# A residual stored to the output early, an MLP result added by accumulating DMA, left sums of the first token blocks made a stage earlier, and a fifth product of two levels

## The chip, the cores and the metric

The kernel runs on one core of one Trainium2 chip. A core has TensorE (matrix products into PSUM, in eight banks of 128 x 512 float32), VectorE, ScalarE, GpSimd (POOL in the profile), and SyncE (SP), whose instruction queue issues nearly all DMA transfers here. Each engine works through its own queue in order; semaphores tie the queues together. The metric is the time of one execution on the device in microseconds. Three runs of the kernel before took 742.08 to 745.21 us, with a median of 743.17.

## The reference

One transformer block over 2048 tokens of width 1024, all inputs bfloat16: layer norm, linear attention with 32 heads, a residual, layer norm, a gated MLP of width 3584, and a second residual.

```
h   = x + A(layernorm(x))                       # linear attention, output projection wo
n   = layernorm(h)
act = relu(n @ W_gate) * (n @ W_up)             # 2048 x 3584
out = h + act @ W_down                          # 2048 x 1024
```

`h` is needed twice: its normalised form feeds the MLP, and `h` itself is added to the MLP's result at the end.

## The kernel before

**Products of seven.** Every large product is cut into 2 x 2 blocks and done with seven block products in place of eight (Winograd's form of Strassen's scheme): sums and differences of left blocks, the same of right blocks, seven products, and sums of those give the four output blocks. A left operand with blocks a11, a12, a21, a22 (first index: half of the tokens, second index: half of the summed dimension) needs s1 = a21 + a22, s2 = s1 - a11, s3 = a11 - a21 and s4 = a12 - s2; products 1 to 7 have the left forms a11, a12, s4, a22, s1, s2, s3. The class `Quad` (L302) holds the steps of one such group of seven, p1 to p7, and `Quads` (L357) runs one group after the other, with products 4 and 3 of a group placed inside the next one. VectorE makes the sums and takes results out of PSUM, ScalarE copies between PSUM banks ("fork") and to SBUF ("snap").

**Tokens.** 2048 tokens are two halves of 1024, the row blocks of the scheme. Each half is again two blocks of 512 tokens, numbered `s` = 0 and 1. The MLP's width is two halves of 1792, each of `FH` = 14 chunks of 128; the output's width is two halves of 512.

**Stages.** (1) Attention, up to about 217 to 280 us, overlapping the next stage. It makes h tile by tile and stores each to a DRAM scratch tensor `h_dram` (`square`, L1009 to L1017). (2) The up stage: for each chunk `fc` and each `s`, one group of seven (`gu_quad`, L1085) gives four blocks of act, 128 x 512 each, for the two token halves and the two halves of the width. A group is 56 matmuls of 128 x 512. The blocks of s = 0 stay in SBUF (`hh0`, L1082). Those of s = 1 go, together with their sums s1 to s4, to DRAM (`spill`, L1097, into `l_dram`), since SBUF has no room for both. In the second half of this stage VectorE also makes the sums of W_down's blocks chunk by chunk (`wd_sums`, L1195), loads them and stores them to `r_dram` through two sets of buffers. (3) The down stage, from about 582 us: the seven products of act with W_down, in the order 1, 2, 6, 5, 7, 3, 4 (L1428 to L1440).

**The down stage.** Each of its seven products has 1024 tokens (both `s`), 1792 summed and 512 columns. A *shallow* one (`shallow`, L1311) does it plainly: 2 blocks `s`, 4 tiles of 128 tokens, 14 chunks, so 112 matmuls of 128 x 512. A *deep* one (`deep`, L1345) applies the seven-product scheme once more inside: the two `s` are its row halves, the tokens are taken in two groups `g`, and each group has seven products of 2 tiles x 7 chunks, 98 matmuls of 128 x 256. For it VectorE makes four right sums (`inner_rights`, L1324) and four left sums per group (`inner_lefts`, L1335), all 128 x 1792. `DEEP` (L1245) names products 2, 3, 5 and 6. Before a product, its right operand (`right`, 1792 KB, two buffers in turn) and the left operand of s = 1 (`left`, 1792 KB, two buffers in turn) are loaded by SP. The left operand of s = 0 comes from `hh0`; where a sum is wanted, `sums0` (L1305) makes it on VectorE in the down stage: eight instructions of 128 x 3584 in all, for s1, s3, s2 and s4, in place or into a free region.

Running sums are kept in SBUF as float32: `U` from products 1, 6 and 7, `Y` from product 5. Four products end an output quarter `q`: product 2 (q = 0), 7 (q = 3), 3 (q = 1) and 4 (q = 2). In each, `load_h` brings the matching 128 KB of h from `h_dram` (32 loads), h is added, and `store` writes 128 KB to the output through SP (32 stores). In products 2 and 3 VectorE adds h to the base (`keep` and `onto`), in product 7 inside `seven`, and in product 4 ScalarE copies h into the PSUM bank ahead of the matmuls (`seed`).

**What sets the order.** All instructions after the set-up are recorded by `Plan` (L33) and then put out in an order that a planner works out from costs and due times written in its code (`cost`, `take`, `schedule`). TensorE keeps near its program order; for SP and VectorE the planner takes what is ready and due first. So an edit in one place can move instructions of these two queues elsewhere. Each queue is fixed once built. Every instruction is issued through L117, which is why all groups of the profile bear that line; they are told apart by tile and shape.

```
            limit = nodes[pe[first]].nom + self.WINDOW
            i = min(now, key=lambda i: (nodes[i].nom if e == "tensor" else nodes[i].late, i))
```

Of the kernel before, what the change touches and what calls it, by code (L numbers as in the profile page):

```python
# [32 lines left out]
class Plan:  # L33
# [30 lines left out]
    def granules(self, ap):  # L64
        key = (ap.tensor.name, ap.offset, ap.ap, ap.dtype)
        if key not in self.cache:
            (row, _), *dims = ap.ap
            size = self.nbytes(ap)
            starts = [ap.offset % row]
            for step, n in dims[:-1]:  # L70
                starts = [s + step * i for s in starts for i in range(n if step else 1)]
            step, n = dims[-1]
            span = step * (n - 1) + 1
            g = 4 if ap.tensor.name.startswith("tiny") else self.G
            self.cache[key] = (ap.tensor.name, sorted({
                q for s in starts for q in range(s * size // g, ((s + span) * size - 1) // g + 1)}))
        return self.cache[key]
# [12 lines left out]
    def cost(self, eng, op, out, ins, k):  # L90

        n = self.free(out)
        if eng == "tensor":
            return max(n / 2.4, 98.0) if op == "matmul" else 80.0, 160 + self.SEM
        if eng == "sync":
            return (1250.0 if op == "dma_start_transpose" else 500.0), self.wire(out) + 2200.0
        acc = 85.0 if k.get("accum_out") is not None else 0.0
        psum = any(a.space == PSUM for a in ins)
        if eng == "vector":
            narrow = all(self.nbytes(a) == 2 and a.space != PSUM for a in (out, *ins) if self.free(a) > 1)  # L100
            mode = {"tensor_tensor": 2, "tensor_scalar": 4, "memset": 2}.get(op, 1) if narrow else 1
            if ins:
                n = max(n, self.free(ins[0]))
            return n / (0.96 * mode) + 69 + acc, 95 + self.SEM
        if eng == "scalar":
            return n / 1.2 + (51 if psum else 93) + 2 * acc, 105 + self.SEM
        return n * 1.15 + 100, 60 + self.SEM

    def take(self, eng, op, args, k):
# [5 lines left out]
        accumulates = op == "matmul" and not k.get("start", True)  # L115
# [3 lines left out]
        if nodes and nodes[-1].open and op == "matmul":  # L119
            v = nodes[-1]  # L120
            v.hold += hold
        else:
            v = Plan.Node()
            v.eng, v.calls, v.preds, v.hold, v.lat, v.dma = eng, [], set(), hold, lat, 0.0
            if eng == "sync":
                v.dma = self.wire(out)
            nodes.append(v)
# [327 lines left out]
def block_kernel(ctx: ExitStack, tc: tile.TileContext, x, wqkv, wo, wg, wu, wd, out, H: int):  # L455
    nc = tc.nc
# [29 lines left out]
    h_dram = dram.tile([P, ST, D], BF16, name="h_dram")  # L486

    LT = {m: BF16 if m in (1, 2, 4) else FP16 for m in range(1, 8)}
    l_dram = {m: dram.tile([P, FH, SW], LT[m], name=f"l_dram{m}") for m in range(1, 8)}
    r_dram = {m: dram.tile([P, FH, D // 2], FP16, name=f"r_dram{m}") for m in (4, 5, 6, 7)}  # L490
# [463 lines left out]
    class Tile_:  # L954
# [54 lines left out]
        def square(self):  # L1009
            h = self.h  # L1010
            nc.sync.dma_start(out=h_dram[:, self.t, :], in_=h)
# [72 lines left out]

    def gu_quad(s, fc, gw, banks):  # L1085
# [10 lines left out]

        def spill():  # L1097

            (a11, a12, a21, a22), (s1, s2, s4) = hh1, ss1
            s3 = a21.bitcast(FP16)  # L1100
            for o, x, y, op in ((s1, a21, a22, ALU.add), (s2, s1, a11, ALU.subtract),
                                (s3, a11, a21, ALU.subtract), (s4, a12, s2, ALU.subtract)):
                nc.vector.tensor_tensor(out=o, in0=x, in1=y, op=op)
            for m, f in ((2, a12), (6, s2), (5, s1), (7, s3), (3, s4), (4, a22)):
                nc.sync.dma_start(out=l_dram[m][:, fc, :], in_=f)
# [16 lines left out]
        def added(q):  # L1122
            def f(ps, u):
# [5 lines left out]
                if s == 1 and q == 1:  # L1129
                    spill()  # L1130
# [85 lines left out]
    for n, (s, fc) in enumerate(order):  # L1216
# [14 lines left out]
        if 8 <= n < 8 + FH:  # L1231
            wd_sums(n - 8)
        if n == 24:
# [11 lines left out]
    DEEP = (2, 3, 5, 6)  # L1245
# [6 lines left out]
    h_ring = ring_of([190.5 + i for i in range(3)])  # L1252
    o_ring = ring_of([193.5 + i for i in range(2)])
    m_ring = ring_of([195.5 + 2 * i for i in range(4)])
# [22 lines left out]
    def load_h(q, s, tt, n, lo, width):  # L1277
        y = at(h_ring(), [n, width])
        t = tile_no(q, s, tt)
        lo += q % 2 * DW  # L1280
        nc.sync.dma_start(out=y, in_=h_dram[:, t:t + n, lo:lo + width])
        return y

    def store(q, s, tt, lo, width, o):
        t = tile_no(q, s, tt)
        lo += q % 2 * DW
        nc.sync.dma_start(out=of_v[:, t:t + o.shape[1], lo:lo + width], in_=o)
# [17 lines left out]
    def sums0(o, x, y, op):  # L1305

        for g in range(2):
            c = slice(g * 2 * P, (g + 1) * 2 * P)
            nc.vector.tensor_tensor(out=o[:, :, c], in0=x[:, :, c], in1=y[:, :, c], op=op)

    def shallow(m, r, lefts, order, then, seed=None):  # L1311
        for s in order:
            for tt in range(4):
                b = shallow_bank()
                if seed is not None:
                    nc.scalar.copy(out=b, in_=load_h(seed, s, tt, 1, 0, DW)[:, 0, :])
                for f in range(FH):
                    if f == FH - 1:
                        nc.cut()
                    nc.tensor.matmul(b, lhsT=lefts[s][f][:, tt * P:(tt + 1) * P], rhs=r[:, f, :],  # L1320
                                     start=(seed is None and f == 0), stop=(f == FH - 1), skip_group_check=True)
# [23 lines left out]
    def deep(m, r, x1, src, dst=None, q=None, with_h=None):  # L1345
# [4 lines left out]
        def quad(g):  # L1350
            lefts = inner_lefts(L0[m], x1, g)

# [7 lines left out]
            def end(s, v, ps, x):  # L1360
                if q is None:
                    add(dst(s, v, g), pair(ps), x)
                else:
                    o = at(o_ring(), [2, DQ])
                    add(o, pair(ps), x)
                    store(q, s, 2 * g, v * DQ, DQ, o)

            def base(s, v):
                return src(s, v, g) if q is None else with_h(src(s, v, g), q, s, v, g)

            def usnap(A, which):
                b = base(which, 1)
                o = b if q is not None else dst(which, 1, g)
# [10 lines left out]
    def keep(src, q, s, v, g):  # L1384
        o = at(m_ring(), [2, DQ], FP32)
        add(o, src, load_h(q, s, 2 * g, 2, v * DQ, DQ))
        return o

    def onto(src, q, s, v, g):
        add(src, src, load_h(q, s, 2 * g, 2, v * DQ, DQ))  # L1390
        return src
# [5 lines left out]
    def seven(s, tt, b):  # L1397
        add(UM[:, s, tt, :], b, UM[:, s, tt, :])
        h = load_h(3, s, tt, 1, 0, DW)
        o = at(o_ring(), [1, DW])  # L1400
        for v in range(2):
            c = slice(v * DQ, (v + 1) * DQ)
            m = at(m_ring(), [2, DQ], FP32)[:, 0, :]
            add(m, Y(s, v, tt // 2)[:, tt % 2, :], h[:, 0, c])
            add(o[:, 0, c], b[:, c], m)
        store(3, s, tt, 0, DW, o)

    def step(m, src, dst=None, q=None, with_h=None):
        r, z = right(m), left(m)
        if m in DEEP:  # L1410
            deep(m, r, z, src, dst, q, with_h)
# [4 lines left out]
        def then(s, tt, b):  # L1416
# [5 lines left out]
            if q is not None:  # L1422
                store(q, s, tt, 0, DW, o.unsqueeze(1))

        shallow(m, r, [[a[:, f, :] for f in range(FH)] for a in (L0[m], z)], (0, 1),
                seven if m == 7 else then, q if m != 7 else None)

    sums0(L0[5], lq[2], lq[3], ALU.add)  # L1428
    sums0(L0[7], lq[0], lq[2], ALU.subtract)
    step(2, U, q=0, with_h=keep)  # L1430

    sums0(L0[6], L0[5], lq[0], ALU.subtract)
    step(6, U, U)
    sums0(L0[3], lq[1], L0[6], ALU.subtract)
# [4 lines left out]
    step(3, Y, q=1, with_h=onto)  # L1439
    step(4, U, q=2, with_h=onto)  # L1440
# [53 lines left out]
```

## Time and profile before

| | |
|---|---|
| median of three runs | 743.17 us (742.08 to 745.21) |
| the profiled execution's own time | 744.89 us |
| its span in the profile | 743.1 us |
| TensorE busy, matmuls | 722.2 us, 3858 |
| VectorE busy | 531.8 us |
| ScalarE busy | 278.6 us |
| POOL busy | 43.7 us, all before 300 us |
| bytes moved by DMA | 110.01 MB in 138707 packets |
| granted TensorE clock | 0.998 of full speed |
| small store to the output, from issue to landing | 1.8 us median, 32 of 128 KB |
| small load of h | 2.4 us median, 32 of 128 KB, 11.9 at most |
| left operand of 1792 KB from l_dram | 7.5 us median |
| right operand of 1792 KB from r_dram | 8.9 us median |

The span is what the profiler saw on the core; the execution's own time is a little longer than the span. A row of the timeline or of the groups gives the engine, the operation, the output and inputs with their shapes (partitions x elements), and in brackets how long the engine stood idle before it and what ended that idle time. A row of a stretch gives its length and each engine's busy time with the number of instructions in it. A few matmul records are missing from the trace, so counts of them are slightly low. Consecutive VectorE instructions of 16-bit operands overlap a little, so that a group's busy time is somewhat below count times mean.

### The profile page before, as it was taken

To read this page: it belongs to the slowest core of one execution; us is meant where nothing else is said; L and a number is where in the kernel's file an instruction comes from. 1 tells how busy PE (TensorE), PEld (TensorE's weight loads), DVE (VectorE), ACT (ScalarE), POOL (GpSimd) and SP (SyncE) were. 2 spreads that over 40 slices of the span, in tenths; PEclk is the share of its full clock that TensorE was granted. 3 is DMA by queue.
4 is the path that set the end of the run, shared out by engine and by line. 5 is a ranking of instruction groups with operands and counts; after the bars stand their busy time and mean duration, and the time that the engine had idled before them with its cause. 6 is when DMAs were issued, how large, how long until landed. Compare 5 with 4: busy or idle time off the path is not lost.

```text
span 743.1 us, 10494 instructions
## 1 busy us (share of the span) xinstructions
PE 722.2 (97%) x3858; PEld 371.7 (50%) x3911; DVE 531.8 (72%) x893; ACT 278.6 (37%) x542; POOL 43.7 (6%) x62
## 2 busy tenths in 40 slices
PE   8899999999999999999999999999998999999998
PEld 3344545444444444444444444444443468884763
DVE  6887755786987875676647546668755999997942
ACT  6677645656554443333323233332323110000010
POOL 2223000002201110000000000000000000000000
PEclk9999999999999999999999999999999999999999
DMA  9464503069856630436051141675876854446741
GB/s 302 105 132 86 170 1 127 3 144 266 189 131 152 140 71 8 140 118 203 21 146 53 43 135 37 183 244 172 258 255 224 270 199 135 174 191 244 266 131 52
DMA packets 138707, 110.01 MB, mean 148 GB/s; under 512 B 54176, under 2 KB 126368, under 8 KB 137248
## 3 DMA queue, kind: packets, MB, share of 16 engines
q1 hardware_dynamic: 138656, 109.34, 50.4%
q8 instruction: 30, 0.49, 0.3%
q14 instruction: 21, 0.17, 0.1%
HBM read 68.68 MB, written 28.57 MB: 131 GB/s over the span
## 4 chain that ended last, share of the span: by engine, by line
PE 64%; DMA 4%; DVE 2%; issue 1%; SPq 1%; ACT 0%; DVEq 0%; ACTq 0%
PE psum L117 64%; DMA mem<-in_B_W_down_dram 2%; DVE mem L117 2%; DMA r_dram<-mem 1%; DMA l_dram<-mem 1%; SPq L117 1%; ACT mem L117 0%; DVEq L1489 0%; DVEq L117 0%; ACTq L117 0%
## 5 line engine op out<-in xcount | busy, mean ns | idle before, releaser
L117 PE MATMUL psum<-mem 128*128 128x512 f16 (+4 forms) x3842 | 721.1, 348 | 16.0 <-DVE mem L117 5.9
L117 PEld LDWEIGHTS <-mem 128*128 128x128 f16 (+1 forms) x3911 | 371.7, 98 | 367.3 <-issue 15.5
L117 DVE TENSOR_TENSOR mem<-psum,mem 128x1024 bf16<-128x1024 f32 (+3 forms) x252 | 185.2, 753 | 143.3 <-ACT mem L117 81.5
L117 DVE TENSOR_TENSOR mem<-mem 128x512 f16<-128x512 bf16 (+8 forms) x332 | 207.4, 663 | 15.4 <-DMA mem<-in_B_W_down_dram 5.2
L117 ACT COPY mem<-psum 128x512 f32<-128x512 f32 (+2 forms) x120 | 90.4, 754 | 209.5 <-PE psum L117 199.7
L117 ACT COPY psum<-psum 128x512 f32<-128x512 f32 (+1 forms) x62 | 45.7, 736 | 154.6 <-PE psum L117 132.3
L117 ACT ACTIVATE mem<-psum 128x512 bf16<-128x512 f32 x90 | 53.6, 597 | 17.9 <-PE psum L117 17.0
L117 DVE SCALAR_TENSOR_TENSOR mem<-mem 128x512 bf16<-128x512 bf16 (+1 forms) x71 | 58.0, 817 | 1.4
L117 DVE SCALAR_TENSOR_TENSOR mem<-psum,mem 128x512 bf16<-128x512 f32 x66 | 45.4, 688 | 15.4 <-PE psum L117 10.3
L117 POOL TENSOR_SCALAR mem<-mem,tiny 128x1024 bf16<-128x1024 bf16 x30 | 38.0, 1266 | 191.9 <-ACT tiny L117 143.2
L117 DVE TENSOR_SCALAR mem<-mem 128x512 bf16<-128x512 bf16 (+1 forms) x49 | 19.3, 393 | 24.4 <-ACT mem L117 24.1
L117 ACT ACTIVATE mem<-mem,tiny 128x1024 bf16<-128x1024 bf16 x25 | 28.6, 1145 | 14.1 <-DVE tiny L117 8.2
L117 ACT ACTIVATE mem<-mem 128x1024 bf16<-128x1024 f32 (+1 forms) x24 | 25.3, 1055 | 4.9 <-DVE mem L117 3.8
L117 ACT ACTIVATE tiny<-tiny 128x1 f32<-128x1 f32 (+2 forms) x112 | 22.3, 206 | 7.8 <-DVE tiny L117 5.1
L117 DVE TENSOR_TENSOR mem<-psum,tiny 128x384 bf16<-128x384 f32 (+1 forms) x48 | 22.8, 507 | 2.6 <-ACT tiny L117 2.0
L117 ACT ACTIVATE tiny<-psum 128x12 f32<-128x12 f32 (+1 forms) x48 | 8.1, 171 | 16.2 <-PE psum L117 16.0
L117 ACT CAST psum<-mem 128x512 f32<-128x512 bf16 x8 | 4.7, 590 | 24.4 <-DMA mem<-h_dram 13.3
L117 ACT CAST mem<-psum 128x512 bf16<-128x512 f32 x18 | 10.5, 582 | 3.2 <-PE psum L117 2.5
L117 DVE BATCH_NORM_STATS2 tiny<-mem 128x6 f32<-128x512 bf16 x14 | 9.2, 678 | 2.2 <-DMA mem<-in_A_x_dram 2.2
L117 POOL TENSOR_SCALAR tiny<-tiny 128x1 f32<-128x1 f32 x14 | 4.2, 300 | 36.7 <-ACT mem L117 23.4
L117 ACT ACTIVATION_READ_ACCUMULATOR mem<-mem,tiny 128x1 f32 x25 | 4.7, 188 | 0.0
L117 DVE TENSOR_SCALAR tiny<-tiny 128x1 f32<-128x1 f32 x16 | 3.4, 211 | 0.4
(18 smaller groups left out, 13.5 us busy)
## 6 DMA issues: line engine op xcount, KB each, us to landing
l_dram<-mem SPq DMA_DIRECT2D x98, 128.0 KB, 2.2
mem<-l_dram SPq DMA_DIRECT2D x6, 1792.0 KB, 7.5
mem<-in_A_x_dram SPq DMA_DIRECT2D x32, 256.0 KB, 3.1
mem<-in_B_W_gate_dram SPq DMA_DIRECT2D x14, 512.0 KB, 4.1
mem<-in_B_W_up_dram SPq DMA_DIRECT2D x14, 512.0 KB, 5.2
mem<-in_B_W_down_dram SPq DMA_DIRECT2D x28, 256.0 KB, 3.5
r_dram<-mem SPq DMA_DIRECT2D x56, 128.0 KB, 2.6
mem<-r_dram SPq DMA_DIRECT2D x4, 1792.0 KB, 8.9
```

The lines of the kernel that those rows point to most:

```text
L117: call = lambda: getattr(getattr(self.nc, eng), op)(*args, **k)
```

## The change

1. **h goes to the output.** `square` stores each tile of h to the output tensor in place of `h_dram`, which is gone. `load_h`, where it is still used, reads it from there.
2. **Results are added by DMA.** `store` has a new argument. With it set, GpSimd issues a DMA that adds the bfloat16 result to what the output holds (`accum_op=ALU.add`); without it, SP stores as before. All results of products 2, 7 and 3 and those of group 0 of product 4 are added this way, 28 transfers of 128 KB. Group 1 of product 4 still loads h (4 loads), adds it on VectorE and stores plainly (4 stores). `keep`, `onto` and the seeding of PSUM are gone; in product 2 the snap writes to a scratch tile (`scratch_u`).
3. **Left sums of s = 0 are made in the up stage.** `spill` takes `s` and is called for both. For s = 0 it makes the four sums of each chunk (4 instructions of 128 x 512), leaves s3 in place of a21, and stores s1, s2 and s4 to the new DRAM tensors `s_dram` 5, 6 and 3 (3 x 14 stores of 128 KB). Chunks 0 to 3, which are made in another way early in the stage, get theirs at turns 9 to 12. In the down stage `left0` loads each of the three back (1792 KB), and `sums0` is gone.
4. **Product 4 becomes deep**, as the fifth.
5. Rings are resized: h buffers 3 to 2, result buffers 2 to 5, scratch 4 to 3. The planner learns the cost of a GpSimd DMA, that an accumulating one reads its target, and to tell rows of a DRAM tensor apart.

The diff, cut to its core:

```diff
@@ Plan
-            starts = [ap.offset % row]
+            starts = [ap.offset % row + ap.offset // (128 * row) * (128 * row)]
...
+        if op == "dma_start" and eng == "gpsimd":
+            return 1000.0, 2.0 * self.wire(out) + 4500.0
...
-        accumulates = op == "matmul" and not k.get("start", True)
+        accumulates = k.get("accum_op") is not None or op == "matmul" and not k.get("start", True)
@@ square
-            nc.sync.dma_start(out=h_dram[:, self.t, :], in_=h)
+            nc.sync.dma_start(out=of[self.t * P:(self.t + 1) * P, :], in_=h)
@@ up stage
+    s_dram = {m: dram.tile([P, FH, SW], FP16, name=f"s_dram{m}") for m in (3, 5, 6)}
...
+    def spill(s, fc):
+        a11, a12, a21, a22 = (hh0(q, fc) if s == 0 else hh1[q] for q in range(4))
+        s1, s2, s4 = ss1
+        s3 = a21.bitcast(FP16)
+        for o, x, y, op in ((s1, a21, a22, ALU.add), (s2, s1, a11, ALU.subtract),
+                            (s3, a11, a21, ALU.subtract), (s4, a12, s2, ALU.subtract)):
+            nc.vector.tensor_tensor(out=o, in0=x, in1=y, op=op)
+        if s == 0:
+            for m, f in ((5, s1), (6, s2), (3, s4)):
+                nc.sync.dma_start(out=s_dram[m][:, fc, :], in_=f)
+        else:
+            for m, f in ((2, a12), (6, s2), (5, s1), (7, s3), (3, s4), (4, a22)):
+                nc.sync.dma_start(out=l_dram[m][:, fc, :], in_=f)
...
-                if s == 1 and q == 1:
-                    spill()
+                if q == 1:
+                    spill(s, fc)
...
+        if 9 <= n < 13:
+            spill(0, n - 9)
@@ down stage
-    DEEP = (2, 3, 5, 6)
+    DEEP = (2, 3, 4, 5, 6)
...
-    h_ring = ring_of([190.5 + i for i in range(3)])
-    o_ring = ring_of([193.5 + i for i in range(2)])
-    m_ring = ring_of([195.5 + 2 * i for i in range(4)])
+    h_ring = ring_of([190.5 + i for i in range(2)])
+    o_ring = ring_of([192.5 + i for i in range(5)])
+    m_ring = ring_of([197.5 + 2 * i for i in range(3)])
...
-    def store(q, s, tt, lo, width, o):
+    def store(q, s, tt, lo, width, o, onto_h):
         t = tile_no(q, s, tt)
         lo += q % 2 * DW
-        nc.sync.dma_start(out=of_v[:, t:t + o.shape[1], lo:lo + width], in_=o)
+        dst = of_v[:, t:t + o.shape[1], lo:lo + width]
+        if onto_h:
+            nc.gpsimd.dma_start(out=dst, in_=o, accum_op=ALU.add)
+        else:
+            nc.sync.dma_start(out=dst, in_=o)
...
-    def sums0(o, x, y, op):
-        for g in range(2):
-            c = slice(g * 2 * P, (g + 1) * 2 * P)
-            nc.vector.tensor_tensor(out=o[:, :, c], in0=x[:, :, c], in1=y[:, :, c], op=op)
+    def left0(m):
+        nc.sync.dma_start(out=L0[m], in_=s_dram[m][:, :, :])
...
-                if seed is not None:
-                    nc.scalar.copy(out=b, in_=load_h(seed, s, tt, 1, 0, DW)[:, 0, :])
...
+            with_h = last and g == 1
...
-                    store(q, s, 2 * g, v * DQ, DQ, o)
+                    store(q, s, 2 * g, v * DQ, DQ, o, not with_h)
...
             def base(s, v):
-                return src(s, v, g) if q is None else with_h(src(s, v, g), q, s, v, g)
+                x = src(s, v, g)
+                if with_h:
+                    add(x, x, load_h(q, s, 2 * g, 2, v * DQ, DQ))
+                return x
...
-            m = at(m_ring(), [2, DQ], FP32)[:, 0, :]
-            add(m, Y(s, v, tt // 2)[:, tt % 2, :], h[:, 0, c])
-            add(o[:, 0, c], b[:, c], m)
-        store(3, s, tt, 0, DW, o)
+            add(o[:, 0, c], b[:, c], Y(s, v, tt // 2)[:, tt % 2, :])
+        store(3, s, tt, 0, DW, o, True)
...
-    sums0(L0[5], lq[2], lq[3], ALU.add)
-    sums0(L0[7], lq[0], lq[2], ALU.subtract)
-    step(2, U, q=0, with_h=keep)
-    sums0(L0[6], L0[5], lq[0], ALU.subtract)
+    left0(5)
+    step(2, U, scratch_u, q=0)
+    left0(6)
     step(6, U, U)
-    sums0(L0[3], lq[1], L0[6], ALU.subtract)
+    left0(3)
     step(5, U, Y)
     step(7, U)
-    step(3, Y, q=1, with_h=onto)
-    step(4, U, q=2, with_h=onto)
+    step(3, Y, Y, q=1)
+    step(4, U, U, q=2, last=True)
```

## The prediction

> **What bounds the kernel now.** I read the busy shares first, then the stretches of the down stage, then TensorE's own timeline, then what VectorE did ahead of the one gap.
>
> ```profile
> PE 722.2 (97%) x3858; PEld 371.7 (50%) x3911; DVE 531.8 (72%) x893; ACT 278.6 (37%) x542; POOL 43.7 (6%) x62
> ```
>
> TensorE is busy 97% of the span. An edit pays only if it takes TensorE work away or closes one of its gaps; VectorE, ScalarE and DMA count where TensorE waits for them. The stretches below are cut where a product of the down stage should begin, worked back from the last matmul at 739.5 (columns: stretch, length, busy PE, weight loads, DVE, ACT, POOL with counts, granted clock, DMA share, GB/s).
>
> ```profile
> 581.90:606.10 24.20, 24.10 (x120) 11.73 (x121) 24.01 (x23) 4.73 (x9) 0.00 (x0) 1.00 0.68 229
> 606.10:627.20 21.10, 21.10 (x195) 18.88 (x194) 18.85 (x23) 1.67 (x3) 0.00 (x0) 1.00 0.42 137
> 627.20:648.20 21.00, 21.00 (x195) 18.77 (x193) 19.59 (x23) 1.14 (x2) 0.00 (x0) 1.00 0.51 197
> 648.20:669.30 21.10, 21.08 (x191) 18.41 (x189) 18.91 (x27) 0.57 (x1) 0.00 (x0) 1.00 0.54 199
> 669.30:693.50 24.20, 24.20 (x117) 11.25 (x116) 20.78 (x42) 0.00 (x0) 0.00 (x0) 1.00 0.61 211
> 693.50:715.30 21.80, 21.02 (x186) 17.95 (x184) 17.89 (x26) 2.19 (x4) 0.00 (x0) 1.00 0.74 254
> 715.30:739.60 24.30, 24.20 (x120) 11.43 (x117) 6.54 (x17) 3.67 (x7) 0.00 (x0) 1.00 0.27 84
> ```
>
> These are products 1, 2, 6, 5, 7, 3, 4. A shallow one (1, 7, 4) takes 24.2 us, a deep one 21.0 to 21.1, and TensorE is full in all but the sixth, though VectorE is at 18 to 24 us in each but the last. POOL does nothing. The two gaps inside are these:
>
> ```profile
> 561.12 150.21 PE L117 MATMUL psum<-mem 128*128 128x512 f16 x1064 [2.70 <-ACT mem L117]
> 712.11 27.39 PE L117 MATMUL psum<-mem 128*128 128x256 f16 x140 [0.78 <-DVE mem L117]
> ```
>
> Ahead of the first, ScalarE's copy at 560.06 waited 6.01 us for VectorE, and VectorE's own queue shows why; ahead of the second it sat on a load of h:
>
> ```profile
> 555.25 0.76 DVE L117 TENSOR_TENSOR mem<-mem 128x512 f16<-128x512 bf16 x2 [2.21 <-DMA mem<-in_B_W_down_dram]
> 555.93 0.68 DVE L117 TENSOR_TENSOR mem<-psum,mem 128x512 bf16<-128x512 f32 x1
> 557.03 0.42 DVE L117 TENSOR_TENSOR mem<-mem 128x512 f16<-128x512 bf16 x1 [0.42 <-DMA mem<-in_B_W_down_dram]
> 558.07 0.76 DVE L117 TENSOR_TENSOR mem<-mem 128x512 f16<-128x512 bf16 x2 [0.61 <-DMA mem<-in_B_W_down_dram]
> ...
> 707.44 0.69 DVE L117 TENSOR_TENSOR mem<-mem 128x512 f32<-128x512 f32 x1 [1.56 <-DMA mem<-h_dram]
> ```
>
> In its fixed order VectorE stands before weight sums whose loads have not landed: 2.21 + 0.42 + 0.61 = 3.24 us late, of which TensorE feels 2.70.
>
> **Product 4 made deep.** It drops 8 x 14 = 112 matmuls of 128x512 and issues 2 groups x 7 products x 2 tiles x 7 chunks = 196 of 128x256. Wide: an up-stage quad is 56 matmuls in 12.09 us on the chain (one begins at 318.47, the next at 330.56), 215.9 ns each. Narrow: 21.0 us over the 195 recorded in the third stretch, 107.7 ns. So 24.18 becomes 21.11: **-3.1 us**. Two rules of one page bear on this. The Trainium skill's "TensorE: Matmul & The Clock Gate", section "Back-to-back issue gap", says that a stream of weight load and matmul runs at about 131 ns for 512 columns and 81 for 128; at those paces (an estimate) 112 wide ones would take 14.7 us and 196 narrow ones at least 15.9, and the edit would lose over 1 us. Its isolated gap, 518 cycles against 262 at 2.4 GHz, gives 24.2 against 21.4, -2.8. This trace contradicts the first pair and agrees with the second; I take the trace's own rows. The 84 extra weight loads stay under the matmuls: deep stretches hold 18.4 to 18.9 us of them in 21.
>
> VectorE's share of product 4 grows: 12 sums of 128x1792 at 1.083 us (4 right, 8 left) = 13.0, 12 evacuations of 128x512 at 0.685 = 8.2, four additions of h at 0.685 = 2.7; it loses 16 evacuations at 0.37 = 6.0. ScalarE loses the eight copies that seeded PSUM (4.7 us busy; their 13.3 us of waiting for h cost nothing) and gains two forks at 0.57. The right sums are the tight point. The load of r_dram4 needs a slot that product 7 frees; it went out at 694.22, and such a load lands in 8.9 us, at 703.1. In the new order VectorE meets those sums after the fourth result of product 3's first quad, some 5 products x 14 x 0.108 = 7.5 us after 693.5 or at 701 to 702. Behind them stand that quad's last two results, whose banks TensorE wants within two products. Cost 0 to 2 us; I take 0, because the right sums of products 6 and 5, between the same sort of quads, made no TensorE gap.
>
> **h taken out of the path.** 16 stores of h go to another address in the same size: nothing. 28 of 32 loads of h and 28 of 32 result stores leave SP's queue; VectorE loses 16 additions of 128x512 at 0.685 (11.0) and 16 of 128x256 at 0.414 (6.6), the latter in product 7. No h is loaded in product 3, so the 0.78 us gap at 711 loses its cause: **-0.8 us** (0 if the right sums above take its place).
>
> **Accumulating stores.** 28 of 128 KB go to POOL's queue, behind nothing: its last work is in the attention stage. No row shows one. Nearest is the plain store, 1.8 us median to landing; it reads its target too, so add a load of h, 2.4: 4.2 us, an estimate. Low end 1.8; high end 11.9, the slowest small load. VectorE waits on them through the five result buffers: a deep quad fills four per 10.5 us, a shallow product one per 3.0, so a buffer is wanted again after about 13 to 15 us. Under that the price is nothing; above it every result behind VectorE's wait is late, then the PSUM bank, then TensorE. The Trainium skill's "SBUF — State Buffer", sections "SBUF: two separate sides" and "Who interferes with whom", warns that a DMA issued by GpSimd has its descriptors written by GpSimd's cores, locked out while VectorE runs in a two-port mode. By that, with VectorE at 18 to 20 us in 21, stores could wait for its pauses, and the loss would be that of the slow rival below. The same section says that a tensor-tensor operation has no such mode, and every VectorE row of the down stage is TENSOR_TENSOR. I take 0.
>
> **First-half sums moved into the up stage.** The down stage loses eight sums of 128x3584 at 2.02 us = 16.1; the stretch 581.9 to 606.1 carried most of them and TensorE was full there, so by itself this gives nothing. The up stage gains 14 x 4 sums of 128x512 at 0.42 = 23.7 us of VectorE, and SP 42 stores at some 0.4 us = 17 us and 5.5 MB. The built program has the same TensorE order until product 4 and the same ScalarE order until its last copies; only VectorE's and SP's queues differ. In the three busiest quads before, VectorE held 9.8, 11.0 and 10.1 us of 12.1; about four more sums in two of them bring 11 to 12, still under TensorE. Bound: nothing, up to 1.7 us more lateness per full quad. The last weight sums keep their place against the quads, with the same loads ahead, so the 2.70 us gap **stays, 0**; the DMA traffic around it (about 260 GB/s) rises by 0.39 MB per 24 us, some 6%.
>
> Three loads of 1.8 MB are new. That of s_dram6 overwrites the a11 block, so SP waits at it until product 1 has read it; behind it stand the last store of s_dram3 and the load of r_dram6, which waited for the same product before (issued at 604.48). At 7.5 + 8.9 us in turn both are there by 621, product 6 begins at 627.2, and its first four left and four right sums (8 x 1.083 = 8.7 us) are wanted only after three product slots of 1.5 us, at 631.7. s_dram3 goes out after the loads for product 5, with 20 us of cover. VectorE's net in the down stage is 23.9 - 39.7 = -15.8 us. Hidden: 0; without that cover, up to 2 us per late load.
>
> **The end.** The last result now leaves in one addition of 0.69 us where two overlapped in 0.76, and its store stays on SP: 0.
>
> **The sum.** 743.1 - 3.1 - 0.8 = 739.2 of span. The profiled execution took 744.89, 1.8 around the span; the median of the runs is 743.17, 1.7 below it. On the median: 743.17 - 3.9 = **739.3**.
>
> **Rivals.** (a) The up-stage gap shrinks or closes, since a store in another place lets the weight loads go earlier: up to -2.7, 736.6 to 738.3. For: it comes from queue order alone, which is rewritten. Against: the sums stand where they stood. (b) VectorE becomes the bound in the full quads and the gap grows by 1.2 to 4: 740.5 to 743.3. For: 94% full there, waiting in order for loads. Against: it has slack in the quads after them, at 7 to 8 us of 12.1. (c) Slower: the accumulating stores hold the result buffers. Five buffers give one store per L/5; deep quads ask one per 2.63 us. At L = 16 us, 20 deep stores lose 0.57 each and 8 shallow ones 0.18: +12.8, 752. It decides from about 15 us (20 x 0.37 = 7.4, back at 746.7). Against: a queue of its own with 1.8 us neighbours. (d) The change does not do what it says: product 4's inputs come too late and its 3.1 us are spent waiting: 742.4.
>
> **How the numbers follow.** Likeliest case 52%, own range 738.4 to 740.4; (a) 24%, (b) 16%, (c) 5%, (d) 3%. A measurement of this kernel tells about 0.5% from no change: below 739.45 is faster, above 746.9 slower. The likeliest falls below in 6 of 10: 0.31 + 0.24 = 0.55 faster; slower is (c), 0.05; same 0.40. The range takes in (a) and (b) with 0.6 and 0.2 us beyond: 736.0 to 743.5, leaving out (c) and tails.
>
> **What would show it.** 196 narrow matmuls from about 712 on, the last stretch about 21 us; no gap waiting for h near 711; the gap before 561 still 2 to 3.5 us; accumulating stores landing in 3 to 6 us and no VectorE wait for out_dram above 1 us; VectorE's busy time over the down stretches near 126.6 - 15.8 = 111 us. I am wrong if TensorE shows a new gap over 1 us in products 3 or 4, if the 561 gap moves by more than 1.5 us, or if stores take over 13 us.

## The result, and the profile after

The changed kernel took 739.70 us (median of 4 runs, 737.91 to 740.14), the kernel before 743.38 us beside it (4 runs, 742.08 to 745.21). The ratio is 0.9944, with a 95% interval of 0.9917 to 0.9971: faster by 0.56%, just past what this kernel's measurement can tell from no change. The forecast was 739.3.

The profiled execution after took 740.07 us with a span of 738.3. TensorE's timeline from 300 us to the end (start, busy us, engine, line, operation, count, and in brackets the gap before it and what ended it):

```profile
299.66 258.95 PE L122 MATMUL psum<-mem 128*128 128x512 f16 x1178
559.92 174.48 PE L122 MATMUL psum<-mem 128*128 128x512 f16 x1288 [1.32 <-ACT mem L122]
```

The gap at 561 is now at 560 and has shrunk from 2.70 to 1.32 us. The gap of 0.78 us near 711 is gone: from 559.92 to 734.40, TensorE's last matmul, it never stops. The down stage by products 2, 6, 5, 7, 3, 4, cut as before (the stretch of product 1 is left out):

```profile
604.70:625.80 21.10, 21.10 (x196) 18.90 (x195) 15.46 (x20) 1.71 (x3) 6.68 (x6) 1.00 0.81 219
625.80:646.90 21.10, 21.10 (x196) 18.91 (x194) 19.64 (x25) 1.14 (x2) 3.15 (x3) 1.00 0.87 277
646.90:668.00 21.10, 21.10 (x193) 18.63 (x191) 12.01 (x16) 0.57 (x1) 0.00 (x0) 1.00 0.51 190
668.00:692.20 24.20, 24.20 (x117) 11.29 (x116) 20.34 (x33) 0.00 (x0) 5.46 (x7) 1.00 0.68 183
692.20:713.30 21.10, 21.10 (x196) 18.91 (x195) 18.49 (x25) 1.71 (x3) 7.49 (x7) 1.00 0.82 226
713.30:734.40 21.10, 21.10 (x194) 18.67 (x191) 14.44 (x20) 0.57 (x1) 8.52 (x7) 1.00 0.57 63
```

The last row is product 4, now deep: 194 recorded matmuls in 21.10 us, where 24.2 stood. TensorE is full in all six. VectorE (third pair) is busy 100.4 us in these rows; with product 1's 14.89 (580.50 to 604.70) that is 115.3, where 126.6 stood and 111 was forecast. GpSimd (fifth pair) now works here: it issues the accumulating stores. Their group, the DMA row with size and median us from issue to landing, and the spread of the landing:

```profile
L122 POOL DMA_DIRECT2D out_dram<-mem x28 | 31.3, 1185 | 422.9 <-DVE mem L122 420.4
...
out_dram<-mem POOLq DMA_DIRECT2D x28, 128.0 KB, 4.4
...
DMA to landing us min/median/max: 3.0/4.4/14.1
```

In the mean one costs GpSimd 1.185 us to issue; in the median it lands after 4.4 us, the slowest after 14.1. In the list of VectorE's waits of the down stage no wait for the output tensor stands.

So the forecast of the whole was nearly met. The experiments show that it was met for reasons that the sum of the prediction does not hold.

### The profile page after: what moved, and what is told of

It is laid out like the page before. It is cut to its first block, busy times and chain, and to the rows that moved or that the text cites. A ratio compares the mean times of both kernels' runs of the same rounds, so it can differ in the third digit from the quotient of the medians.

```text
span 738.3 us, 10739 instructions
## 1 busy us (share of the span) xinstructions
PE 720.2 (98%) x3942; PEld 380.9 (52%) x3995; DVE 538.8 (73%) x921; ACT 275.2 (37%) x536; POOL 75.4 (10%) x90
## 4 chain that ended last, share of the span: by engine, by line
PE 63%; DMA 3%; DVE 2%; issue 1%; SPq 1%; ACT 0%; DVEq 0%; ACTq 0%
PE psum L122 63%; DVE mem L122 2%; DMA mem<-in_B_W_down_dram 2%; DMA r_dram<-mem 1%; SPq L122 1%; ACT mem L122 0%; DMA l_dram<-mem 0%; DVEq L122 0%; ACTq L122 0%
## 5 line engine op out<-in xcount | busy, mean ns | idle before, releaser
L122 PE MATMUL psum<-mem 128*128 128x512 bf16 (+4 forms) x3926 | 719.3, 343 | 13.8 <-DVE mem L122 5.1
L122 PEld LDWEIGHTS <-mem 128*128 128x128 bf16 (+1 forms) x3995 | 380.9, 98 | 353.2 <-issue 14.9
L122 DVE TENSOR_TENSOR mem<-psum,mem 128x1024 bf16<-128x1024 f32 (+3 forms) x248 | 188.2, 772 | 124.4 <-ACT mem L122 70.1
L122 DVE TENSOR_TENSOR mem<-mem 128x512 f16<-128x512 bf16 (+6 forms) x364 | 212.2, 620 | 21.6 <-PE psum L122 7.7
L122 POOL DMA_DIRECT2D out_dram<-mem x28 | 31.3, 1185 | 422.9 <-DVE mem L122 420.4
L122 DVE TENSOR_SCALAR mem<-mem 128x512 bf16<-128x512 bf16 (+1 forms) x49 | 19.3, 393 | 24.7 <-ACT mem L122 24.4
```

The costliest lines, as they stand in the source:

```text
L122: call = lambda: getattr(getattr(self.nc, eng), op)(*args, **k)
```

## The experiments

Every kernel was timed beside the kernel before on the same chip. Three parts are told apart: D, the deep product 4; M, the sums of the first token blocks moved into the up stage; A, the residual in the output with accumulating stores. All eight combinations, as ratio to before with the 95% interval, and the median in us:

| | without A | with A |
|---|---|---|
| neither | 1 (743.2 to 743.4) | 0.9987 [0.9977, 0.9996], 742.49 |
| D | 0.9996 [0.9985, 1.0007], 743.27 | 0.9958 [0.9946, 0.9970], 740.37 |
| M | 1.0101 [1.0074, 1.0127], 749.67 | 0.9979 [0.9967, 0.9992], 741.86 |
| D and M | 1.0078 [1.0058, 1.0098], 749.63 | 0.9944 [0.9917, 0.9971], 739.70 (the change) |

**Parts taken away from the kernel after.** First product 4 made shallow again:

```diff
-    DEEP = (2, 3, 4, 5, 6)
+    DEEP = (2, 3, 5, 6)
...
+            with_h = last and s == 1
...
+                if with_h:
+                    add(x, x, h[:, c])
```

> The changed kernel with product 4 shallow again; the residual by accumulating DMA and the moved sums stay. The second block of tokens of product 4 loads h, adds it on VectorE and stores plainly, so that the tail is a plain store. Theory: TensorE gets 112 wide matmuls for 196 narrow ones, 24.2 us for 21.1, so +3.1 us on the changed kernel, 742.8, with no other gap in TensorE. Rival (the gain is in VectorE and SP and not in the narrower product): less than +1.5, under 741.2.

Measured: 741.86 us, between theory (742.8) and rival (under 741.2). Its TensorE timeline:

```profile
560.33 177.26 PE L122 MATMUL psum<-mem 128*128 128x512 f16 x1204 [1.14 <-ACT mem L122]
```

From the gap to the end TensorE works 177.26 us instead of 174.48: 2.8 more, of 3.1 predicted. The spans of the two profiled executions differ by 3.1 (741.4 and 738.3), the medians by 2.2.

Next the accumulating stores were taken away, with D and M kept: before's h loads, additions and plain stores.

```diff
+    s_dram = {m: dram.tile([P, FH, SW], FP16, name=f"s_dram{m}") for m in (3, 5, 6)}
...
-                if s == 1 and q == 1:
-                    spill()
+                if q == 1:
+                    spill(s, fc)
...
-    DEEP = (2, 3, 5, 6)
+    DEEP = (2, 3, 4, 5, 6)
...
-    sums0(L0[5], lq[2], lq[3], ALU.add)
-    sums0(L0[7], lq[0], lq[2], ALU.subtract)
+    left0(5)
```

> The changed kernel's deep product 4 and moved sums, but h in a scratch tensor, 32 loads of h by SP, h added on VectorE (28 times 128x512 or its equal) and plain stores, with the rings of the kernel before. Theory: only the gap on a late load of h comes back, +0.8 us on the changed kernel, 740.5; VectorE has the room (its busy time from 582 on rises from about 115 to about 135 us in 152). Rival (VectorE becomes the bound in the deep products in a row): TensorE waits several times in products 2, 3 and 4, +3 us or more, over 742.7.

Measured: 749.63 us, slower than before. My expectation fell by 9 us. TensorE's timeline, and the stretch behind its longest gap (columns as in the stretches above; the granted clock is the third number from the end):

```profile
623.68 90.05 PE L117 MATMUL psum<-mem 128*128 128x256 f16 x686 [4.91 <-DVE mem L117]
715.71 27.67 PE L117 MATMUL psum<-mem 128*128 128x256 f16 x252 [1.98 <-DVE mem L117]
...
623.68:629.00 5.32, 5.32 (x26) 3.76 (x26) 4.28 (x6) 0.00 (x0) 0.00 (x0) 0.50 0.26 74
```

A gap of 4.91 us opens in product 2, one of 1.98 where 0.78 stood, and the granted clock is half around the end of the longer one: cut finer, from 622.6 to 629.4. The 26 matmuls there stand where 49 of 107.7 ns would.

Then M was taken away, A and D kept:

```diff
-                if q == 1:
+                if s == 1 and q == 1:
                     spill(s, fc)
...
-        if 9 <= n < 13:
-            spill(0, n - 9)
...
-    left0(5)
+    sums0(L0[5], lq[2], lq[3], ALU.add)
+    sums0(L0[7], lq[0], lq[2], ALU.subtract)
```

> The changed kernel's deep product 4 and accumulating stores, but the eight sums of 128x3584 for the first token block made on VectorE in the down stage, as before. Theory: they are hidden under product 1 and nothing follows in the down stage; the gap near 560 goes back to about 2.7 us if it was the moved sums that changed the queue order there (+1.4, 741.1), and stays at 1.3 if it was the missing loads of h (739.7). Rival (VectorE is the bound): new TensorE gaps in products 2, 6 or 5 and over 742.

Measured: 740.37 us, between the two cases of the theory, and no gap in the down stage. The gap at 560 is longer in this profile:

```profile
561.48 174.48 PE L122 MATMUL psum<-mem 128*128 128x512 f16 x1288 [2.34 <-ACT mem L122]
```

**Single parts on the kernel before.** D alone is one line:

```diff
-    DEEP = (2, 3, 5, 6)
+    DEEP = (2, 3, 4, 5, 6)
```

> The kernel before with product 4 made deep and nothing else. Theory: the parts add up, so -3.1 us on the kernel before, 740.3, with the gap of 0.8 us near 711 still there. Rival (the other two parts are what makes room for it): VectorE, at about 145 us busy in 155 us of the down stage, makes TensorE wait in products 3 and 4, and less than half of the 3.1 us is left, 742 or more.

Measured: 743.27 us, no different from before. TensorE, and VectorE ahead of its gap:

```profile
708.35 27.67 PE L117 MATMUL psum<-mem 128*128 128x256 f16 x252 [1.98 <-DVE mem L117]
```

```profile
699.35 1.42 DVE L117 TENSOR_TENSOR mem<-psum,mem 128x512 f32<-128x512 f32 x2 [0.22 <-PE psum L117]
700.68 3.81 DVE L117 TENSOR_TENSOR mem<-mem 128x512 f32<-128x512 f32 x4
704.41 0.68 DVE L117 TENSOR_TENSOR mem<-psum,mem 128x512 f32<-128x512 f32 x1
```

The second row is VectorE's additions of h: four in a row, between two results of product 3 and just where the sums of a deep product 4 have to come in. They take 3.81 us, where four at 0.685 are 2.7; why they took longer is not shown. The longer gap accounts for 1.2 of the lost 3 us. Another 0.7 stands behind TensorE's last matmul: 4.3 us to the end of the span, 3.6 before. Most of the rest goes with the clock. A mean granted clock of 0.998 or less is found in 15 of this kernel's 22 runs and in 23 of the 55 of before; the other runs average 741.7 and 742.6 us. So where no clock is lost D alone gains 0.9 us. Where its runs lose it is not shown: the profiled execution was one of those without loss before the end.

M alone:

```diff
+                if q == 1:
+                    spill(s, fc)
...
+        if 9 <= n < 13:
+            spill(0, n - 9)
...
-    sums0(L0[6], L0[5], lq[0], ALU.subtract)
+    left0(6)
```

> The kernel before with only the eight first-half sums moved into the up stage (14 x 3 stored tiles, three loads of 1.8 MB in their place); product 4 stays shallow, h still travels through its own buffer and VectorE still adds it. Theory A (the move costs nothing and pays only by the order it leaves in the up stage): the gap at 561 falls from 2.70 to about 1.3 us, the 0.78 us gap at 711 stays; 742.0. Theory B (the loads of the spilled sums come late for VectorE as long as it and the DMA queues also carry h, as in the kernel without accumulating stores): a gap of 4 to 5 us in product 2 or 6 followed by a stretch at half clock; 746 or more.

Measured: 749.67 us, theory B by its number; whether late loads are the reason is asked below. The profiled execution took 755.55 us, the slowest of six (the others 748.2 to 750.4). The gap in product 2 is the same 4.91 us. TensorE's timeline, and VectorE ahead of the gap:

```profile
629.05 93.00 PE L117 MATMUL psum<-mem 128*128 128x256 f16 x714 [4.91 <-DVE mem L117]
```

```profile
615.01 1.42 DVE L117 TENSOR_TENSOR mem<-psum,mem 128x512 f32<-128x512 f32 x2 [0.84 <-PE psum L117]
616.46 0.69 DVE L117 TENSOR_TENSOR mem<-mem 128x512 f32<-128x512 f32 x1
618.02 3.10 DVE L117 TENSOR_TENSOR mem<-mem 128x1792 f16<-128x1792 f16 x3 [0.87 <-DMA mem<-s_dram]
622.65 4.22 DVE L117 TENSOR_TENSOR mem<-mem 128x1792 f16<-128x1792 f16 x4 [1.53 <-PE psum L117]
626.79 0.69 DVE L117 TENSOR_TENSOR mem<-psum,mem 128x512 bf16<-128x512 f32 x1
```

VectorE takes four results of product 2, adds one tile of h, and then stands at seven sums of product 6 (128x1792), the next product, before it takes the fifth result. They wait 0.87 us for the spilled sums' load and 1.53 us for TensorE, and last until 626.87; TensorE meanwhile needs the bank of that result. In the kernel after, the order at this place is one result, one sum:

```profile
613.99 0.69 DVE L122 TENSOR_TENSOR mem<-psum,mem 128x512 bf16<-128x512 f32 x1 [1.64 <-PE psum L122]
614.59 1.08 DVE L122 TENSOR_TENSOR mem<-mem 128x1792 f16<-128x1792 f16 x1
615.59 0.68 DVE L122 TENSOR_TENSOR mem<-psum,mem 128x512 bf16<-128x512 f32 x1
```

A alone, made from the kernel after by undoing D and M as above:

> The kernel after with product 4 shallow again and the eight first-half sums back in the down stage, so that of the change only the residual put into the output early and the accumulating stores are left. Theory A (they pay for the gap at 711 alone): that gap goes, 0.78 us, the gap at 561 stays at 2.3 to 2.7; 742.4. Theory B (they also make the room that lets other parts pay, but pay nothing by themselves): no gap in the down stage, and 742.9 to 743.3, no different from before. Wrong if a gap of over 1 us shows in the down stage.

Measured: 742.49 us, 0.1% below before. No gap is left in the down stage, the one at 560 stays (2.60 us). Theory A.

**Order or load?** Two runs ask why M fails without A. The first keeps M alone and all its loads, and changes only the order in which the planner may put VectorE's queue: each sum of product 6 waits, in the planner, for a result of product 2.

```diff
+    results, sums = [], []
+    def after_result():
+        sums.append(len(nc.nodes) - 1)
+        nc.nodes[-1].preds.add(results[min(4 + len(sums), len(results)) - 1])
...
             nc.vector.tensor_tensor(out=o, in0=a, in1=b, op=op)
+            if m == 6:
+                after_result()
```

> The kernel with only the moved sums (749.7), and one thing more: in VectorE's queue each of product 6's twelve sums is kept behind a result of product 2, as the kernel after has them, where the planner had put seven of them ahead of one result. TensorE's and ScalarE's order stay as they were, and so does what is loaded. Theory A (the order of VectorE's queue makes the 4.91 us gap): no gap over 1 us in products 2 and 6, and no stretch at half clock behind it, 749.7 - 4.9 - 3.4 = 741.4, at most 743.2. Theory B (the loads of the spilled sums land late, whatever the order): the gap stays at 3 to 5 us or moves to the start of product 6, 747 or more.

Measured: 744.16 us, ratio 1.0012 [1.0002, 1.0022]. Each against before on its own chip, M alone lost 6.2 us and this loses 0.9: 5.3 came back by order alone. TensorE, and VectorE at the gap that is left:

```profile
620.78 90.28 PE L117 MATMUL psum<-mem 128*128 128x256 f16 x714 [1.10 <-DVE mem L117]
```

```profile
617.88 0.69 DVE L117 TENSOR_TENSOR mem<-mem 128x512 f32<-128x512 f32 x1 [5.19 <-DMA mem<-h_dram]
618.49 0.68 DVE L117 TENSOR_TENSOR mem<-psum,mem 128x512 bf16<-128x512 f32 x1
```

The 4.91 us gap is down to 1.10, and no half clock follows. What is left is a load of h. SP issued it at 606.71, behind the two loads of spilled sums (599.26) and that of r_dram (603.58), 5.5 MB in all; VectorE waited 5.19 us for it, until 617.88. So theory A holds for the size of the loss, though its bound of 743.2 was missed by 1 us. The lateness of loads is real too, but it is small, and it falls on h.

The second run is the one with product 4 shallow, with h taken out altogether (its output lacks the residual) and plain stores in SP's queue:

```diff
-        if onto_h:
-            nc.gpsimd.dma_start(out=dst, in_=o, accum_op=ALU.add)
-        else:
-            nc.sync.dma_start(out=dst, in_=o)
+        nc.sync.dma_start(out=dst, in_=o)
...
-            with_h = last and s == 1
+            with_h = False
```

> The kernel after with product 4 shallow, every result stored plainly from SP's queue and the residual added nowhere in the down stage (so the output lacks it): no load of h, no addition of h, and no accumulating store. Beside it stand the same kernel with accumulating stores (741.9) and the one with h loaded and added (749.7). Theory A (it is the loads and additions of h that leave no room for the moved sums): no gap in the down stage, 741.5 to 742.3. Theory B (the result stores in SP's queue, ahead of the loads of the next product, take the room, and POOL's queue is what gives it): a gap of 2 us or more in products 2 to 3, and 745 or more.

Measured: 741.98 us, as against 741.86 with accumulating stores in its place. TensorE has no gap behind 558.39. Theory A: what the accumulating stores give the moved sums is the absence of h from SP's and VectorE's queues. Which queue carries the results does not matter here. The loads of h and its additions are not told apart.

**The slower rival, made to happen.** Two result buffers instead of five:

```diff
-    o_ring = ring_of([192.5 + i for i in range(5)])
+    o_ring = ring_of([192.5 + i for i in range(2)])
```

> The kernel after with two result buffers instead of five, so that in a deep product of the last three a buffer is wanted again after some 5.3 us, while addition, issue and landing of its accumulating store take 0.7 + 1.2 + 4.4 = 6.3 us. If the landing time is what sets reuse (the slower rival of the prediction, made to happen): each of 16 deep stores beyond the first holds VectorE about 0.5 us, and as the results of a quad come in bunches, 1 to 3 us, some of it taken up by VectorE's slack of 5 us per product; VectorE rows that wait for out_dram show in products 3 and 4; 739.7 to 743. If the store lets go of its buffer before it has landed, no such waits and 739.7. Over 745 only if a gap of some us brings a stretch at half clock with it.

Measured: 771.09 us, far past my 739.7 to 743. From VectorE's list of waits from 600 us on (total, times, longest), the first of these waits, and of TensorE's timeline two of its gaps:

```profile
DVE mem L122 <- DMA out_dram<-mem: 7.8, 5, 2.0
...
744.53 0.69 DVE L122 TENSOR_TENSOR mem<-psum,mem 128x512 bf16<-128x512 f32 x1 [1.85 <-DMA out_dram<-mem]
```

```profile
723.90 7.17 PE L122 MATMUL psum<-mem 128*128 128x256 bf16 x49 [4.64 <-DVE mem L122]
...
759.08 1.69 PE L122 MATMUL psum<-mem 128*128 128x256 f16 x14 [2.59 <-DVE mem L122]
```

A buffer is let go only when its store has landed: VectorE waits five times, up to 2.0 us. But the first of these waits begins at 742.7, and by then seven of TensorE's nine gaps from 621 us on have passed, 16.0 of 19.3 us, with three stretches at half clock behind them. Waits for a buffer did not make those. The planner, which knows the ring, had also put VectorE's queue in another order (three and four sums ahead of single results at 613.86 and 618.15, much as with M alone) and changed the end of TensorE's. So the price of a full ring is shown in kind, and it is the smaller part of the 31 us; that the new order is the rest is argued, since no run changes the ring and keeps the order.

**Versions meant to be faster.** Product 1 deep as well, a sixth of two levels:

```diff
+    X10, X11 = at(72, [FQ, SW]), at(188, [FQ, SW])
...
-    shallow(1, r1, ([lq[0][:, f, :] for f in range(FH)], z1), (1, 0),
-            lambda s, tt, b: nc.scalar.copy(out=UM[:, s, tt, :], in_=b))
+    def deep1():
+        rights = inner_rights(r1, [79, 195, 198.5])
...
+        for g in range(2):
+            quads.run(quad(g))
```

> The kernel after with product 1 of the down stage made deep as well (a sixth product of two levels): its 112 wide matmuls become 196 narrow ones, its sums for the first group are made in space that the up stage has freed, and ScalarE copies its results. Theory A (TensorE stays full and the time is that of its matmuls): 24.2 becomes 21.1 us, 736.6. Theory B (VectorE, which already waits on late weight sums at 554 to 562, has not finished the twelve sums and the first results of product 1 in time): a gap of 2 us or more at 560 to 585, with half clock behind it; 739 to 745, the gain gone as in the kernel with the deep product 4 alone.

Measured: 760.10 us, theory B in kind and far past its range. VectorE now waits 22.2 us for weight loads in nine waits between 480 and 600 us; in the kernel after it is 3.0 in three. SP issues the last of these loads at 570.47, where the kernel after issues its last at 551.66. Of VectorE's timeline the longest wait, of TensorE's the gap that it makes and the longest one, ahead of which VectorE waited 5.03 us for a store of spilled sums:

```profile
558.85 0.42 DVE L122 TENSOR_TENSOR mem<-mem 128x512 f16<-128x512 bf16 x1 [8.43 <-DMA mem<-in_B_W_down_dram]
```

```profile
561.29 5.34 PE L122 MATMUL psum<-mem 128*128 128x512 f16 x24 [3.38 <-DVE mem L122]
...
638.88 11.29 PE L122 MATMUL psum<-mem 128*128 128x256 bf16 x76 [7.14 <-DVE mem L122]
```

Nine gaps from 541 to 639 us sum to 22.4 us.

Two runs went for the last gap, of 1.32 us. The first makes loads and sums of the weights of products 4 to 7 due 12 us earlier in the planner:

```diff
+            nc.push = -12000.0
             wd_sums(n - 8)
+            nc.push = 0.0
```

> The kernel after with the loads and sums of the weights of products 4 to 7 due 12 us earlier in the planner, so that VectorE no longer meets a weight load that has not landed at 554 to 557; TensorE's and ScalarE's order stay the same. Theory A (that lateness is all of the last gap of 1.32 us at 560): no gap over 0.3 us between 300 and the end, 739.7 - 1.3 = 738.4. Theory B (VectorE is full in those stretches, so that the sums only push the results back elsewhere): another gap of 1 to 3 us between 450 and 600, 739.7 to 742.

Measured: 749.84 us. The gap at 560 is gone, and eight others stand between 498 and 559, 8.0 us in all; theory B, and beyond its range. The second moved only the loads, by 3 us:

```diff
+            nc.push = -3000.0
             nc.sync.dma_start(out=at(kb + 2 * k, [2, DW]),
                               in_=wd_v[:, k * FH + c, :].rearrange("p (h d) -> p h d", h=2))
+            nc.push = 0.0
```

> The kernel after with only the loads of the weights of products 4 to 7 due 3 us earlier in the planner, not their sums: in SP's queue they now go out by twos between the stores that free their slots, where they went out by fours behind up to seven stores. TensorE's, ScalarE's and GpSimd's order stay the same. Theory A (the last gap of 1.32 us is the lateness of those loads): VectorE waits on them under 1 us in 545 to 560 and no gap over 0.4 us is left at 560; 738.5. Theory B (as when loads and sums both came early, VectorE then meets a sum that holds up a result somewhere else): other gaps of 1 to 3 us between 450 and 560 and 740 to 745.

Measured: 751.52 us, worse than either theory. TensorE's timeline, and VectorE ahead of its first long gap:

```profile
539.79 25.13 PE L123 MATMUL psum<-mem 128*128 128x512 f16 x106 [5.12 <-ACT mem L123]
...
570.67 176.07 PE L123 MATMUL psum<-mem 128*128 128x512 f16 x1288 [3.65 <-ACT mem L123]
```

```profile
529.19 0.42 DVE L123 TENSOR_TENSOR mem<-mem 128x512 f16<-128x512 bf16 x1 [1.38 <-DMA mem<-in_B_W_down_dram]
532.53 0.42 DVE L123 TENSOR_TENSOR mem<-mem 128x512 f16<-128x512 bf16 x1 [2.92 <-DMA mem<-in_B_W_down_dram]
```

The loads now go out by ones and twos, and VectorE, whose order the planner changed with them, waits for several of them. A shift of 3 us in 28 due times cost 12 us, with TensorE's order untouched. Nothing tried beats the kernel after.

## Why the prediction was right and where it was wrong

- **Product 4 made deep, -3.1 us.** Right in mechanism, provided A is there: the last stretch is 21.10 us with narrow matmuls at 107.7 ns, and the right sums, the tight point, made no gap. The size was nearly right: 2.8 us of TensorE's time and 3.1 of span in the profiles, 2.2 in the medians (741.86 to 739.70; without M, 742.49 to 740.37).
- **h taken out of the path, -0.8 us.** Right: the gap at 711 went, and A alone measures 1.0 us (0.9987). What the step did not price is its larger part: h's loads and additions also held the room that the two other parts need.
- **Accumulating stores, 0.** The price was right: no VectorE wait with five buffers. The landing was right only in the median, 4.4 us where 4.2 were estimated. It went with the load on the DMA engines: a median of 7.8 us in products 2 and 6 (DMA share 0.81 and 0.87) and 6.9 in product 3 (0.82), outside the 3 to 6 forecast, and 3.7 and 3.6 in products 7 and 4 (0.68 and 0.57). The slowest, 14.1 us, is past the 13 us that the prediction had named as a sign of being wrong, and even that held nothing up. VectorE did not keep the stores back: in product 3, with VectorE busy 18.49 of 21.10 us, seven went out and TensorE was full. Since every VectorE row there is TENSOR_TENSOR, the lockout that the prediction weighed was not put to the test. Two buffers do make VectorE wait, as the slower rival says; five are enough.
- **First-half sums moved.** "The 2.70 us gap stays, 0" failed in the profile: it is 1.32. That the move did it is not shown. In seven profiles with M and the same order of VectorE's and SP's queues in the last 15 us up to the gap it is 3.21, 1.96, 1.32, 1.32, 1.14, 0.64 and, with two buffers, nothing; in the four without M it is 2.70, 2.60, 2.34 and 1.77. The average is lower with M, 1.4 as against 2.4 us, a part of rival (a), but one order gives very different gaps. By medians M gives 0.6 to 0.7 us where A is there, which is not clear of noise. I had also written "the sums stand where they stood" against that rival; their place against the loads did not stay.
- **"Hidden: 0; without that cover, up to 2 us per late load."** This step had the mechanism wrong. It looked for the price in the loads' lateness, and with M alone the load of s_dram6 was late by 0.87 us only. The price was the queue's order: with h also in the queues, the planner put seven of the sums that read loaded tiles ahead of one result, and without A that costs 4.91 us of TensorE and a half clock behind it. Busy time taken off VectorE was not the cover that mattered: M alone takes 16.1 us of sums off it in the down stage and was the slowest of the three parts.
- **The sum.** It added the parts as if they were independent. Measured alone they are worth -0.3, -1.0 and +7.5 us (0.9996, 0.9987 and 1.0101 of 743.4), together +6.2; the whole is -4.2. The forecast of 739.3 was close because all three parts came together, which the argument never used. And the closeness is in part luck: put in one after the other as A, M and D, the medians give 0.9 + 0.6 + 2.2 = 3.7 us where 0.8 + 0 + 3.1 = 3.9 was forecast, so that a term set at nothing made up for one set too high. In the profiles, which both have 3.4 us at half clock near 28 us, the span fell by 4.8 us: 3.1 by product 4, 0.8 by the gap at 711, 1.4 by the gap at 560, with 0.2 given back ahead of that gap and 0.3 behind TensorE's last matmul.

Open: what sets the length of the gap at 560. It was 0 to 3.21 us in the kernels with this order of TensorE's work up to there, and both attempts to close it by earlier loads opened others.

## What to carry to other kernels

Where engines run fixed queues, price a group of edits as a group: ask for each part which other part clears the queue that it needs, and look at the new order of VectorE's queue around every TensorE handover, not only at the sums of busy time. Taking a stream of small loads and additions out of the queues can be worth little by itself and still be what makes the other edits pay. Before fixing a short gap by shifting loads, count what stands behind every wait that the shift creates; where the load on VectorE is high, a few microseconds of order can cost ten. And do not give a difference of one or two microseconds between two profiles to an edit before other profiles of the same order have shown how far it moves by itself.

## What was not expected of the hardware

A gap can cost more than its length. Behind the 4.91 us gap the granted clock was 0.50 from 622.6 to 629.4 us with D and M, and from 628.1 to 634.9 with M alone: 6.8 us, of which 5.7 to 5.9 lie behind the gap and cost half of that, 2.9 us, on top. Behind the gap of 5.12 us in the last run it was half for 3.4 us.

Length alone does not decide. Gaps of 2.14 us (early weights, half from 556.4 to 559.8) and 3.21 us (M alone at 562, half from 563.2 to 566.6) were followed by half clock; the 2.70 us of before and 3.38 us with product 1 deep, both at 561, were not. Clearest is a stop of TensorE in the attention stage that no edit touches, 2.07 or 2.08 us before it resumes at 26.5 to 27.6. It stands in twelve of the fourteen profiles: in seven some 3.4 us at half clock follow, in five none do. Here are before and A alone (the clock is the third number from the end):

```profile
27.60:30.90 3.30, 3.08 (x9) 1.14 (x9) 2.53 (x5) 2.41 (x6) 1.43 (x2) 0.55 0.00 0
27.60:30.90 3.30, 3.30 (x16) 1.47 (x15) 2.73 (x6) 3.28 (x8) 1.43 (x2) 1.00 0.00 0
```

Such a stretch costs 1.7 us. It explains much of why runs of one kernel differ: of the 55 runs of before beside the first experiments, the 32 with a mean granted clock of 0.999 or more average 742.6 us, the 23 with less 744.6.

The Trainium skill's "TensorE: Matmul & The Clock Gate", section "What's actually happening", describes a gate that halves the clock after an idle window of 3413 ns and says that the window runs freely. The lengths of the half stretches agree with that: 3.4 us, 6.8 behind 4.91 us, and 10.2 behind the 7.14 us of product 1 deep are one, two and three windows. But a gap of 2.07 or 2.14 us is too short to hold an idle window wherever it lies, and half clock followed it; there the measurement goes against the page's words. What decides instead is open.

A small load behind large ones on SP's queue lands late: the four loads of h that the kernel after keeps, issued behind loads of 1792 KB (two at 667.9, two from 694.6 on), take 10.9 us (median), as against 2.4 for the 32 of before. Neither TensorE nor VectorE waited for them here; GpSimd did once, 2.5 us.
